# Fourier mixing and a hard-swish MLP on one core: batch 0's first two stages on the later batches' tables

## The chip, the cores and the metric

The kernel runs on one core of a Trainium2 chip. The core has five engines that run side by side and wait for one another by semaphores: TensorE (PE in the profile, with its weight loads listed as PEld), VectorE (DVE), ScalarE (ACT), GpSimd (POOL) and SyncE (SP). In this kernel SP only issues transfers (DMAs); ACT and POOL issue some too. The metric is the device time of one execution in microseconds. Three executions of the kernel before took 2608.43, 2608.70 and 2608.97 us; the median is 2608.7 us.

## The reference

```python
def _attn_ref(x, filt_r, filt_i):          # x: (8, 3008, 256), filters: (1505, 256)
    X = np.fft.rfft(x, axis=1)
    F = (filt_r + 1j * filt_i)[None, :, :]
    return np.fft.irfft(X * F, n=x.shape[1], axis=1).astype(np.float32)

def _moe_ref(x, w_in, w_out):              # x: (24064, 256), w_in: 256 x 2048, w_out: 2048 x 256
    h = x @ w_in
    g = h * np.clip(h + 3.0, 0.0, 6.0) / 6.0
    return (g @ w_out).astype(np.float32)
```

Each of the 8 batches is transformed along its 3008 rows, multiplied by one complex filter per frequency and channel, and transformed back. The 24064 rows that result go through a two-layer MLP with a hard swish. All is float32.

## The kernel before

3008 is 47 x 64, so a row number is written n = 64a + c with a < 47 (`NA`) and c < 64 (`NC`), and c = 32h + j with h in {0, 1} and j < 32 (`HC`). The forward transform has two stages. Stage A sums over a and leaves 24 residues k of the frequency (`KH`), real and imaginary. Stage B sums over c and leaves, for each k, 64 frequencies q. Then come the product with the filter (`f_unit`, on VectorE), the inverse of stage B (`bi_unit` on TensorE, copied out by ScalarE and stored to a scratch array `g_tmp`), and the inverse of stage A (`n_first`, `n_five`, `n_unit`, which read `g_tmp` back into `t4`). Their result is the ring `xn`, from which the MLP takes blocks of 512 rows: `plain_up` and `plain_down` for block 0, a form with fewer products for the others. The MLP fills TensorE for nearly all the time; the transform of batch n + 1 is put between the MLP steps of batch n by a written plan. Batch 0 has nothing to hide behind: its whole forward transform runs ahead of the MLP, and it is this opening, the first 64 us, that the change is about.

The opening is written out in order (a manual schedule: every engine gets its instructions in the order of the program text). In the kernel before:

- `x0_load` (L405) loads batch 0 into the upper part of the weight array `w_all` (`x0_at`), as 96 partitions (2a + h, starting at partition 16) in six transfers on SP (L1031). `start_t`, `wi_t` and the memsets of the 16 partitions below come first (L985 to L1023). ACT issues `start_t` as its first instruction.
- `keep_warm` (L1026) runs two products on zeros.
- `a0_unit(j)` (L417), for four values of j at a time and for each half of the 256 channels, runs four 112 x 128 x 128 products. The data are the stationary operand and one small table (`start`) the moving one; the table keeps the two h apart and has no factor that depends on j. One copy per half, on ACT or DVE, writes the results to `zt`, that is `xn` and `xs`.
- `table_load` (L255) loads the filter rows for four residues k (a chunk `c`, six chunks), in pieces of 32 partitions, and the chunk's part of a table `wb`, a 128 x 128 matrix for each k, which holds what stage A left out. Chunks 0 and 1 go to the tiles `ft0`, `ft1` and to `wa`; chunks 2 to 5 over `x0`, when stage A is through with it.
- `turn(c)` (L426) transposes eight 128 x 128 blocks of `zt` on TensorE; two copies bring them to `t2`.
- `b_unit(0, i)` (L532, L549) multiplies two k by their own 128 x 128 table into one PSUM bank; `f_unit(0, i)` (L552, L561 to L563) makes three DVE products; `bi_unit` (L577, L584) makes the inverse products of the chunk before, `g_store` stores them from POOL.
- For the last chunk `y_unit` combines the products, `direct` (L732) takes them straight to the first rows, `g0_first` (L621) and `first_load` (L659) carry the rest through `g_tmp`, and `n_first` (L736) ends the opening.
- Later `wa` (stage A's table for the later batches) and `wf` (their stage B table) are loaded, L1072, L1073 and L1084.

The conversions of the MLP weights (`w_load` L317, `w_conv` L327) are spread over the opening: transfers of 0.5 MB on SP, eight DVE instructions each for the first.

The transfers that SP and ACT issue share eight semaphores in turn, so an issue also waits until the transfer eight places before it has landed; SP issues strictly in order.

The later batches do stage A otherwise (`a_unit`, `a6_unit`): h = 0 lies on partitions 0 to 46 and h = 1 on 64 to 110, `wa` has 48 columns for each j with the j-dependent factors in it, four products run in the four quarters of the array, and DVE makes the sum and the difference of the two h. Their stage B (L540) then needs one table `wf` for all k, in pieces of 64 x 32.

## Time and profile before

| | |
|---|---|
| median of three executions | 2608.7 us |
| span of the profiled execution (first to last instruction) | 2607.0 us |
| around the span, to the median | 1.7 us |
| PE busy | 2591.8 us, 99% of the span |
| DVE busy | 2053.9 us, 79% |
| ACT busy | 1295.6 us, 50% |
| POOL busy | 486.7 us, 19% |
| start of `n_first` on PE | 61.62 us |
| moved by DMA in the first 61.6 us | 240 GB/s on average |

Times below are microseconds from the start of the span. In the timeline a line is a run of like instructions on one engine: start, duration, engine, line, operation, what it writes from what, partitions x elements, the number of records, and in brackets the idle time before it with what ended it. A float32 product makes two records. Idle time of PE is what costs, as PE is busy for 99% of the span; what stands in the opening shifts all that follows.

### The profile page before, as it was taken

Reading aid. Unit: us, or ns where it says so; the run is one execution under the profiler, and the core shown is the slowest. Engines: PE = TensorE matmul, PEld = TensorE weight load, DVE = VectorE, ACT = ScalarE, POOL = GpSimd, SP = SyncE. Lnnn points to the kernel's source line nnn. Section 1 sums busy time; section 2 is a strip of 40 time slices with the busy share of each in tenths; the row PEclk is TensorE's granted clock in tenths of the full one; section 3 lists DMA queues with packets and bytes.
Section 4 is the critical chain, followed back from the end, with each engine's and each line's share of the span. In section 5 each row is a group of like instructions: output and inputs, shape, how many; then the busy total and the mean of one; then the engine's idle time right before and its main releaser. Section 6 shows DMA issues by size and latency. Waiting matters only on the chain.

```text
span 2607.0 us, 86613 instructions
## 1 busy us (share of the span) xinstructions
PE 2591.8 (99%) x37708; PEld 2051.0 (79%) x37708; DVE 2053.9 (79%) x3611; ACT 1295.6 (50%) x2677; POOL 486.7 (19%) x711
## 2 busy tenths in 40 slices
PE   8999999999999999999999999999999999999999
PEld 6487777878778787788877888777877778888887
DVE  7978868888788877888778887788877888766666
ACT  4554454545545455444554444545445454455554
POOL 2242021121211202111031210311113120111110
PEclk9999999999999999999999999999999999999999
DMA  8732234112241132411224112331123321110000
GB/s 247 224 92 81 59 101 119 54 33 87 74 123 54 33 87 78 119 54 37 83 83 114 54 38 82 89 108 54 54 66 91 106 57 49 50 44 24 20 22 26
DMA packets 130834, 200.32 MB, mean 77 GB/s; under 512 B 21602, under 2 KB 97472, under 8 KB 130262
## 3 DMA queue, kind: packets, MB, share of 16 engines
q1 hardware_dynamic: 115165, 150.12, 20.4%
q0 software_dynamic: 14720, 44.16, 6.1%
q8 instruction: 296, 4.85, 0.8%
q14 instruction: 84, 0.69, 0.1%
q10 hardware_dynamic: 569, 0.50, 0.1%
HBM read 122.43 MB, written 83.98 MB: 79 GB/s over the span
## 4 chain that ended last, share of the span: by engine, by line
PE 94%; DVE 3%; DMA 2%; POOL 1%; issue 0%; ACT 0%; SPq 0%; POOLq 0%; DVEq 0%; ACTq 0%
PE po L765 43%; PE al L765 24%; PE be L765 18%; PE psn L705 2%; PE psf L540 1%; PE psf L481 1%; PE psf L600 1%; PE be L600 1%; POOL w_all L369 1%; PE be L481 1%; DVE g L818 1%; DMA g_tmp<-t 1%; PE psf L765 0%; DMA ft<-in_filt_i_dram 0%; DVE y L335 0%
## 5 line engine op out<-in xcount | busy, mean ns | idle before, releaser
L765 PEld LDWEIGHTS po<-w_all,g 128*64 128x64 f32 x20808 | 1232.5, 137 | 247.0 <-issue 12.4
L765 PE MATMUL po<-w_all,g 128*64 128x128 f32 (+1 forms) x20808 | 1407.0, 274 | 1.4 <-DVE g L818 0.7
L813 ACT ACTIVATE r<-h,half_c 128x512 f32<-128x512 f32 x736 | 531.0, 722 | 346.7 <-DVE h L794 334.7
L765 PE MATMUL al<-xt,w_all 128*64 128x256 f32 x4416 | 664.0, 379 | 0.4 <-POOL w_all L369 0.3
L818 DVE SCALAR_TENSOR_TENSOR g<-r,h 128x512 f32<-128x512 f32 x736 | 536.2, 730 | 144.6 <-ACT r L813 129.2
L765 PE MATMUL be<-xt,w_all 128*64 128x256 f32 x2944 | 442.6, 379 | 0.0
L794 DVE TENSOR_TENSOR h<-be,s 128x512 f32<-128x512 f32 x368 | 253.8, 690 | 131.3 <-PE be L765 102.2
L760 POOL TENSOR_TENSOR xt<-xn 128x256 f32<-128x256 f32 x184 | 150.7, 838 | 890.3 <-ACT xn L687 890.3
L765 PEld LDWEIGHTS be<-xt,w_all 128*64 128x64 f32 x2944 | 211.3, 137 | 106.5
L765 PEld LDWEIGHTS al<-xt,w_all 128*64 128x64 f32 x4416 | 278.9, 137 | 1.7 <-POOL w_all L369 1.4
L808 ACT ACTIVATE h<-al 128x256 f32<-128x256 f32 x368 | 141.4, 384 | 273.2 <-PE al L765 272.4
L826 DVE TENSOR_TENSOR g<-g 128x512 f32<-128x512 f32 x367 | 261.4, 712 | 12.6
L799 DVE TENSOR_TENSOR h<-al,s 128x256 f32<-128x256 f32 x368 | 156.0, 424 | 135.6 <-PE al L765 130.5
L789 ACT ACTIVATE s<-al 128x256 f32<-128x256 f32 x368 | 141.6, 385 | 207.2 <-PE al L765 207.1
L765 PE MATMUL al<-xn,w_all 128*64 128x256 f32 (+1 forms) x1536 | 240.1, 393 | 1.1 <-DVE g L818 0.7
L765 PE MATMUL be<-xn,w_all 128*64 128x256 f32 (+1 forms) x1536 | 236.4, 388 | 0.0
L780 ACT ACTIVATE s<-be 128x256 f32<-128x256 f32 x368 | 141.4, 384 | 170.1 <-PE be L765 170.1
L825 DVE TENSOR_TENSOR g<-g 128x256 f32<-128x256 f32 x367 | 165.5, 451 | 12.6
L779 ACT ACTIVATE s<-al 128x256 f32<-128x256 f32 x368 | 141.5, 384 | 59.1 <-PE al L765 59.1
L831 DVE TENSOR_TENSOR g<-g 128x256 f32<-128x256 f32 x367 | 161.7, 441 | 2.4
L765 PEld LDWEIGHTS be<-xn,w_all 128*64 128x64 f32 x1536 | 110.3, 137 | 62.3 <-issue 7.4
L506 POOL DMA_DIRECT2D z_tmp<-t x144 | 72.0, 508 | 321.4 <-ACT s L780 296.0
(162 smaller groups left out, 1766.6 us busy)
## 6 DMA issues: line engine op xcount, KB each, us to landing
t<-g_tmp SPq DMA_DIRECT2D x184, 120.0 KB
t<-z_tmp SPq DMA_DIRECT2D x42, 512.0 KB
g_tmp<-t POOLq DMA_DIRECT2D x68, 256.0 KB, 4.3
z_tmp<-t POOLq DMA_DIRECT2D x120, 144.0 KB, 3.7
o_tmp<-o SPq DMA_DIRECT2D x46, 256.0 KB
xs<-in_x_dram SPq DMA_DIRECT2D x60, 192.0 KB
ft<-in_filt_r_dram SPq DMA_DIRECT2D x168, 64.0 KB
ft<-in_filt_i_dram SPq DMA_DIRECT2D x168, 64.0 KB
```

The source lines that it names most:

```text
L760: nc.gpsimd.tensor_tensor(out=o, in0=x0, in1=x1, op=op_)
L765: nc.tensor.matmul(ps[ds(o, STRIP)], w[:, ds(o, STRIP)], x, skip_group_check=True, **kw)
L779: nc.scalar.activation(out=s[:, 0, :], in_=al, func=AXT.Copy)
L780: nc.scalar.activation(out=s5, in_=be[:, 1, :], func=AXT.Copy)
L789: nc.scalar.activation(out=s[:, 1, :], in_=al, func=AXT.Copy)
L794: nc.vector.tensor_tensor(out=st["h"][0].rearrange("p (a n) -> p a n", a=2), in0=be, in1=s, op=ALU.add)
L799: nc.vector.tensor_tensor(out=st["h"][1][:, 256:512], in0=al, in1=s5, op=ALU.add)
L813: nc.scalar.activation(out=r, in_=st["h"][i], func=AXT.Relu, bias=half_c, scale=1.0 / 6.0)
L818: nc.vector.scalar_tensor_tensor(out=st["g", k, p][:, o:o + 2, :].rearrange("p a n -> p (a n)"), in0=st["r", i], scalar=1.0, in1=st["h"][i ...
L825: v.tensor_tensor(out=g[:, G1, :], in0=g[:, G3, :], in1=g[:, G22, :], op=ALU.add)
L826: v.tensor_tensor(out=g[:, G3:G2 + 1:2, :], in0=g[:, G3:G1 + 1, :], in1=g[:, G11:G11 + 1, :].broadcast_to([P, 2, 256]), op=ALU.subtract)
L831: nc.vector.tensor_tensor(out=g[:, G4, :], in0=g[:, G12, :], in1=g[:, G2, :], op=ALU.subtract)
```

## The change

Batch 0's stage A uses `wa` and the four quarters of the array, as the later batches do; ScalarE copies the h = 0 sums to SBUF, and DVE makes even (add) and odd (subtract) sums. Stage B uses `wf`; `wb`, the second half of `start` and the fourth part of `wi` are gone. `x0` lies on partitions 0 to 46 and 64 to 110 and comes in four pieces a group, five groups, each with its columns of `wa`, which now are loaded here and not later. Filter rows come for two chunks at a time, in eight pieces of 16 partitions.

```diff
     def table_load(b, c):
-        if b == 0 and c >= FB:
-            at = x0_at(1536 * (c - FB), 1536)
-            t, wb = at[:, 0:1024].rearrange("p (k d) -> p k d", k=TC), at[:, 1024:].rearrange("p (k m) -> p k m", k=TC)
+        n = TC if b else 2 * TC
+        if b:
+            t = ft[(b * NT + c) % FB]
+            st["ft", b, c] = t
         else:
-            t, wb = ft[(b * NT + c) % FB], wa[:, ds(c % FB * TC * P, TC * P)].rearrange("p (k m) -> p k m", k=TC)
-        st["ft", b, c] = t
...
+            t = x0_at(2 * TC * D * (c // 2 - 1), 2 * TC * D).rearrange("p (k d) -> p k d", k=n) if c else ft_all
+            for i in range(2):
+                st["ft", b, c + i] = t[:, ts(i, TC), :]
         for src, p0 in ((filt_r, 0), (filt_i, HALF)):
-            nc.sync.dma_start(t[p0:p0 + 32, :, :].rearrange("p k d -> p (k d)"),
-                              raw(src, c * TC, [[NA * D, 32], [1, TC * D]]))
-            nc.sync.dma_start(t[p0 + 32:p0 + 64, :, :], raw(src, NA - c * TC, [[NA * D, 32], [-D, TC], [1, D]]))
-        nc.sync.dma_start(wb, wb_d[:, ts(c, TC), :])
-        st["wb", b, c] = wb
+            for r in range(2):
+                o = p0 + 32 * r
+                nc.sync.dma_start(t[o:o + 16, :, :].rearrange("p k d -> p (k d)"),
+                                  raw(src, c * TC + NA * r, [[2 * NA * D, 16], [1, n * D]]))
+                nc.sync.dma_start(t[o + 16:o + 32, :, :],
+                                  raw(src, NA * (2 - r) - c * TC, [[2 * NA * D, 16], [-D, n], [1, D]]))
...
-    def x0_load(j, n):
-        nc.sync.dma_start(x0[X0:XR, j:j + n, :].rearrange("p j d -> p (j d)"), raw(x[0], j, [[HC * D, XR - X0], [1, n * D]]))
+    def x0_load(j, n, q):
+        q.dma_start(wa[:, j * ATOM:(j + n) * ATOM + 16], wa_d[:, j * ATOM:(j + n) * ATOM + 16])
+        for h in range(2):
+            for r, m in ((0, 32), (32, NA - 32)):
+                nc.sync.dma_start(x0[h * 64 + r:h * 64 + r + m, j:j + n, :].rearrange("p j d -> p (j d)"),
+                                  raw(x[0], r * NC + h * HC + j, [[NC * D, m], [1, n * D]]))
...
-    def a0_unit(j):
+    def a0_unit(j, n):
         for dh in range(2):
-            ps = bank(0)
-            for u in range(4):
-                nc.tensor.matmul(ps[:, ts(u, P)], x0[0:XR, j + u, ts(dh, P)], st["start"][0:XR, ts(1, P)],
-                                 start=True, stop=True)
-            copy(dh and j not in (8, 12), zt(dh).rearrange("p (n j) -> p j n", j=HC)[:, j:j + 4, :],
-                 ps.rearrange("p (j n) -> p j n", j=4)[:, :, 0:4 * KH])
+            ps = [bank(0) for h in range(2)]
+            for u in range(n):
+                for g in range(2):
+                    for h in range(2):
+                        nc.tensor.matmul(ps[h][ts(g, HALF), ts(u, ATOM)], x0[ds(h * 64, NA), j + u, ds(dh * P + g * HALF, HALF)],
+                                         wa[ds(h * 64, NA), ts(j + u, ATOM)].rearrange("p (r x k) -> p k r x", r=2, k=2),
+                                         start=True, stop=True)
+            first = sp.tile([P, 512], FP32, name="s1")[:, 0:n * ATOM]
+            nc.scalar.activation(out=first, in_=ps[0][:, 0:n * ATOM], func=AXT.Copy)
+            for s_, op_ in ((0, ALU.add), (1, ALU.subtract)):
+                by_j = lambda t: t.rearrange("p (j q x) -> p j q x", j=n, x=NU)
+                nc.vector.tensor_tensor(out=zt(dh).rearrange("p (s q j x) -> p s j q x", s=2, j=HC, x=NU)[:, s_, j:j + n],
+                                        in0=by_j(first), in1=by_j(ps[1][:, 0:n * ATOM]), op=op_)
 
     def turn(c):
...
-                    k = c * TC + 2 * v + u
-                    nc.tensor.transpose(ps[:, ds(u * D + dh * P, P)], zt(dh)[:, ts(k, P)], st["start"][:, 0:P])
+                    z = zt(dh).rearrange("p (s r x) -> p s x r", s=2, x=NU)[:, s_, 2 * c + v, :]
+                    nc.tensor.transpose(ps[:, ds(s_ * D + dh * P, P)], z, st["start"][:, 0:P])
...
     def b_unit(b, i):
         c, r = divmod(2 * i, TC)
-        if b > 1:
+        if b != 1:
             t = st.pop(("t2", b, c))
             ps = [bank(b) for k in range(2)]
...
-        nc.scalar.dma_start(st["start"][:, 0:2 * P], start_d)
         zero = rp.tile([P, 512], FP32, name="r", tag="r")
-        nc.vector.memset(x0[0:X0, 0:4, :], 0.0)
-        nc.gpsimd.memset(x0[0:X0, 4:8, :], 0.0)
...
-        nc.scalar.dma_start(wi, wi_d)
...
-        for j, n, bits in (0, 4, 0), (4, 4, 0), (8, 8, 1), (16, 8, 1), (24, 4, 1), (28, 4, 1):
-            x0_load(j, n)
-            load_bits(bits)
+        groups_0 = (0, 4), (4, 4), (8, 8), (16, 8), (24, 8)
+        for j, n in groups_0:
+            x0_load(j, n, nc.sync if j else nc.scalar)
+            load_bits(j >= 8)
+            if j == 4:
+                nc.scalar.dma_start(st["start"][:, 0:P], start_d)
+        nc.sync.dma_start(wf, wf_d)
         table_load(0, 0)
+        nc.sync.dma_start(wi, wi_d)
         load_bits(2)
-        table_load(0, 1)
-        for j in range(0, HC, 4):
-            a0_unit(j)
-            convert(j == 4)
+        for j, n in groups_0:
+            a0_unit(j, n)
+            convert(j == 8)
         nc.gpsimd.memset(t4, 0.0)
-        for c in range(FB, NT):
+        for c in range(FB, NT, 2):
             table_load(0, c)
...
             for i in (2 * c, 2 * c + 1):
-                b_unit(0, i)
+                if i % 2 == 0:
+                    b_unit(0, i)
                 f_unit(0, i)
...
-        nc.sync.dma_start(wa[:, 0:528], wa_d[:, 0:528])
-        nc.sync.dma_start(wf, wf_d)
...
-            nc.sync.dma_start(wa[:, 528:], wa_d[:, 528:])
```

The code that makes the tables changes with it (the frequencies of a chunk stand in the order that `wf` gives). Stages of the later batches issue the same instructions as before.

## The prediction

> **What bounds the kernel now.** I read the page first, then the opening engine by engine in the timeline, then the chain that ended last within it. The page's slices: PE is full in all but the first.
>
> ```profile
> PE   8999999999999999999999999999999999999999
> DMA  8732234112241132411224112331123321110000
> ```
>
> PE works for 2591.8 of 2607.0 us, so about 15 us are to be had in all; most of them lie in the first 64. Only there can the change act, and what it shifts there shifts everything behind. The timeline of PE and DVE, opening:
>
> ```profile
> 3.02 3.78 PE L1028 MATMUL al<-r 128*128 128x512 f32 x4 [3.02 <-ACT r L1022]
> 6.59 15.48 PE L421 MATMUL po<-p,w_all 112*128 112x128 f32 x128
> 22.96 0.33 PE L433 MATMUL al<-p,xs 128*128 128x128 f32 x1 [0.53 <-DVE xs L413]
> 24.20 1.99 PE L549 MATMUL po<-t,wa 128*128 128x256 f32 x8 [0.25 <-ACT t L415]
> 51.16 1.81 PE L732 MATMUL psn<-w_all,t 128*128 128x470 f32 x4 [1.02 <-ACT t L587]
> 61.62 1.85 PE L765 MATMUL psn<-wai,t 128*64 128x94 f32 x40 [0.80 <-DMA t<-g_tmp]
> ```
> ```profile
> 25.36 0.69 DVE L561 TENSOR_TENSOR s<-po,ft 128x512 f32<-128x512 f32 x1 [0.69 <-PE po L549]
> 42.78 0.69 DVE L561 TENSOR_TENSOR s<-po,w_all 128x512 f32<-128x512 f32 x1 [0.29 <-PE po L549]
> 47.51 0.69 DVE L561 TENSOR_TENSOR h<-po,w_all 128x512 f32<-128x512 f32 x1 [0.46 <-issue]
> ```
>
> Stage A keeps PE without a gap from 6.59 to 22.07: the loads run ahead of it. From 25.36 DVE makes filter products (4.29 us a chunk) with only the two gaps shown, so PE's 4.66 us a chunk hardly counts: DVE already sets this stretch. The end of the opening, 61.62, waited 0.80 for `g_tmp` to come back. What feeds it, on SP and ACT, and the shape of the chain:
>
> ```profile
> 0.75 1.34 SPq L406 DMA_DIRECT2D w_all<-in_x_dram  x3
> 17.38 0.33 SPq L277 DMA_DIRECT2D ft<-in_filt_r_dram  x1
> 1.17 1.28 ACT L991 ACT_TABLE_LOAD   x1 [1.17 <-PEq L1274]
> 2.77 0.33 ACTq L1023 DMA_DIRECT2D wi<-wi_t  x1
> ```
> ```profile
> 49.87 0.37 ACT t L587
> 50.98 4.56 DMA g_tmp<-t
> 58.19 3.34 DMA t<-g_tmp
> ```
>
> L277 at 17.38 is the issue that waited for the last piece of x0 (eight places before it), so x0 was in at about 17.4. In the stretches table (last columns: granted clock, DMA share, GB/s) DMA is full from 18 to 46:
>
> ```profile
> 18.00:28.00 10.00, 8.60 (x63) 7.49 (x62) 5.71 (x8) 3.84 (x6) 0.00 (x0) 1.00 0.95 248
> 28.00:46.00 18.00, 18.00 (x96) 11.09 (x94) 17.10 (x26) 7.93 (x14) 3.56 (x6) 1.00 0.98 296
> 90.00:97.00 7.00, 6.53 (x114) 3.30 (x110) 6.62 (x12) 3.54 (x6) 0.00 (x0) 1.00 0.73 222
> ```
>
> **The change, part by part.** The same forms run later in the trace, so their prices can be read:
>
> ```profile
> 95.15 1.38 PE L705 MATMUL psn<-wai,t 48*64 48x47 f32 x80
> 426.65 1.09 PE L540 MATMUL psf<-t,wf 64*32 64x512 f32 x16
> ```
>
> 1. Stage A on PE. L705 is the same shape as the new products: 40 quarter products in 1.31 us to the next start, 0.131 us per four. The change has 256, 64 fours: 8.4 us instead of 15.5. But it gains only where PE was the bound, and after the change loading is.
>
> 2. Loading x0. Before x0's last piece there stood 3.15 MB of x0, 0.52 of weights, 0.13 of `start` and 0.13 of `wi`: 3.93 MB from about 1.9 to 17.4, 0.254 MB/us. Now it is 3.08 of x0, 0.81 of `wa`, 0.52 and 0.07: 4.49 MB, 17.7 us at that rate, so 19.6 if the queue never empties. It does, I think. Group j of `wa` takes columns 48j to 48(j + n) + 16, so each load overlaps the one before by 16 columns, and each must wait for it to land. `wa`'s first group is no longer ACT's first act: it stands behind the 1.28 us table load and two activations, at about 2.4. Its landing: `start`, issued at 0.75, let PE's weight load start at 5.74; `wi`, issued at 2.77, was in by 6.67; the `g_tmp` piece took 3.3 us. With 3.0 us it is in at 5.4; only then can SP issue `wa`'s second group and x0's. The third waits again, another 3.0: 8.4. So the first group (0.49 MB) moves until about 4, the second from 6.7 to 8.6, and the third's bytes start near 9.7 (0.4 an issue, and 1.2 to the first bytes, as x0's start at 0.75 with bytes from 1.9 shows): some 4 us of the queue stand empty. The remaining 3.4 MB take 12.1 to 13.4 us (0.28 to 0.254), and x0 is in at 22 to 23; I take 23 because there are more pieces, 0.42 us of SP each. The pieces of 32 and 15 partitions ran at 222 GB/s with DMA only 0.73 busy at 90 to 97, where SP issued each 0.42 us; that would make it 25 as the upper end. Lower end: 19.6, no idling. The fourth and fifth waits lie behind 1.3 MB of queued loads and cost little.
>
> 3. Stage A's end. Last group: 16 fours, 2.1 us; ACT's copy of 384 elements about 0.5 (0.38 for 256, 0.60 for 512); two DVE sums of 384 at 0.56 (0.42 for 256, L799; 0.69 for 512). 23 + 2.1 + 0.5 + 1.1 = 26.7, against first full transposes at 22.96. Sums for the earlier groups and the one conversion (4.4 us) lie in the gaps of loading; DVE's whole work here is 14.0 us (8 x 0.36 + 12 x 0.56 + 4.4) in the 20 from the first group's landing, so it is not the bound. `st["start"]` and the memsets go, at no gain: other engines waited for neither but PE's start at 5.74.
>
> 4. To the first filter product. Before: 2.40 us from 22.96 to 25.36. Now one call makes both banks of the chunk and needs both halves of `t2`, the second being DVE's copy: + 0.5. First product: 26.8 + 2.9 = 29.7, + 4.3. The filter rows for it, 1.05 MB in 16-partition pieces behind x0 and `wf`, need 5.7 us at the 0.21 MB/us that 17.4 to 27.5 had: 28.7, just hidden; late by a microsecond per 0.2 MB if the loads slip further. Chunk 2's rows have 8.6 us more.
>
> 5. Chunks. PE now needs 0.87 (transposes) + 1.03 (L540) + 1.87 (inverse) = 3.8 per chunk, under DVE's 4.29. The gaps of 0.29 and 0.46 close: - 0.7. The last chunk starts at 51.1 instead of 47.51, + 3.6. That is all stage B can give: VectorE's work in it is the same.
>
> 6. Tail. `direct` and the last inverse on PE follow + 3.6; they would have let `n_first` start at 60.82 but for the `g_tmp` wait, so 64.4. By the store: ACT's copies of chunk 4 were held to 49.87 by an earlier store, not by DVE, which had its products at 47.04; now they come about 3 later, and 11.7 us on (49.87 to 61.53) it is 64.5. So + 2.8.
>
> 7. Behind it. `wa` (0.79 MB) and `wf` leave SP's queue at 59.5 to 73; no PE gap there hangs on them alone (the wait at 97.20 is 0.67 for `xs`, behind conversions). 0, at best - 0.7. The rest is the same code.
>
> Sum: + 2.8 on the span of 2607.0, 2609.8. The profiled span stands 1.7 under the median 2608.7; with the same around it, 2611.5.
>
> **Where a rule of the skill speaks.** Trace first: `keep_warm`'s four 512-column passes take 3.78 us, two such passes, side by side, later 0.47 (L584); stage A's first four products took 1.95 us (ACT's first copy 8.54), later ones 0.89, while the granted clock reads 1.00. So PE starts at half speed until about 9. The Trainium skill, "TensorE: Matmul & The Clock Gate", Part 1, says PE falls back to half after some 3.4 us without work. By that rule gaps of 3 to 4 us between x0's groups would leave stage A's end cold; no stretch of this trace has such a gap. By the rule the sum is rival C's, without it A's. My sum goes by full speed, as every row behind 9 us shows it.
>
> **Rivals.**
> - A, as summed: 2611.5, own range 2609.5 to 2613.5. For it: the overlap of `wa`'s columns is in the text. 0.45.
> - B, the loads never idle (the other side): the waits land in 2 us each and the queue stays full. x0 in at 17.7 to 19.6. Break-even is x0 in at 20.2: then the first product comes at 26.9, + 1.5, less 0.7 and the 0.8 of slack. At 18.5 the end is 1.2 to 1.7 earlier: about 2607.5. For it: SP had 2.9 MB out by 5.6; against it: the order of SP's queue. 0.20.
> - C, PE is at half speed again at the end of stage A: last group + 2.1, transposes + 0.9, first stage B + 1.0 on top of A: 2615.5; if the last two groups back to back warm it, 2613. For it: the half-speed start; against it: groups follow each other every 3 to 4 us. 0.20.
> - D, strided reads cost: the transposes now read every twelfth element, the new products every second of `wa`. No PE row has this; the nearest are copies with 128-byte steps (384 elements 0.83 on DVE against 512 plain in 0.69: 1.6 times an element) as the upper end, 1.0 as the lower. I take 1.0 in A; with 1.6 the chunk on PE is 4.3, level with DVE, and stage A's end and first transposes gain 1.6: 2613. 0.15.
>
> **Numbers.** A change under 0.2% (5.2 us) is about what a measurement here cannot tell from none. Faster than 2603.5 needs more than B's best: 0.02. Slower than 2613.9: most of C, a third of D, A's edge: 0.22. The rest 0.76. The range, 2607 to 2616, holds B's middle and C.
>
> **What the profile after would show.** A: SP's second `wa` issue near 5, its third near 8; stage A on PE in five bursts with gaps of 2 to 4 us; first filter product at 29 to 30; chunks 4.3 apart; `n_first` near 64.4. B: first product before 27. C: the last burst of stage A (16 fours, 128 records) lasting 4 us, not 2. D: transposes over 1.2 us a chunk. Wrong would also be a wait behind 64 us that is not there before, or filter rows that land after 30.

## The result, and the profile after

The changed kernel takes 2621.26 us (median of 4 runs, 2620.14 to 2622.10) against 2608.56 for the kernel before in the same comparison: a ratio of 1.0050, 95% interval 1.0035 to 1.0064. It is 12.7 us slower. The prediction was 2611.5 with a range that ended at 2616.

The profiled execution after took 2622.1 us with a span of 2620.3. Its page has the same PE share as before, 99%. In PE's row only the first slice differs; the DMA digits differ by one here and there, along the whole run:

```profile
PE   7999999999999999999999999999999999999999
DMA  8742244212342123421224212241133421110000
```

The first of PE's 40 slices fell from 8 to 7; that is 65 us in which PE worked less. All of the loss lies there. A landmark behind it, the start of each of the 368 operations on DVE that make `h` from `be` and `s` in the MLP steps, comes 13.3 us later than before at the first one (129.98 us before) and 12.4 to 13.2 later at all others; the span ends 13.4 later. So what happened is over by 75 us, and the rest of the run only carries it along.

The opening on PE, from the timeline of the kernel after (start, busy us, line, what, count, and in brackets the idle time before and what ended it):

```profile
6.24 1.53 PE L394 MATMUL po<-wa,w_all 47*64 47x48 f32 x64
9.37 1.14 PE L394 MATMUL po<-wa,w_all 47*64 47x48 f32 x62 [0.68 <-DMA w_all<-in_x_dram]
14.99 3.66 PE L394 MATMUL po<-wa,w_all 47*64 47x48 f32 x126 [1.67 <-DMA w_all<-in_x_dram]
22.01 4.11 PE L394 MATMUL po<-wa,w_all 47*64 47x48 f32 x128 [0.59 <-DMA w_all<-in_x_dram]
27.90 4.00 PE L394 MATMUL po<-wa,w_all 47*64 47x48 f32 x126 [1.79 <-DMA w_all<-in_x_dram]
33.13 0.49 PE L411 MATMUL al<-p,xs 128*128 128x128 f32 x1 [0.81 <-DVE xs L401]
35.78 1.96 PE L518 MATMUL po<-t,wf 64*32 64x512 f32 x16 [0.83 <-issue]
46.26 1.09 PE L518 MATMUL po<-t,wf 64*32 64x512 f32 x16
63.96 2.30 PE L709 MATMUL psn<-w_all,t 128*128 128x470 f32 x4 [2.45 <-issue]
```

Stage A's five groups are to be seen (32 fp32 products of the program are 64 records, a group of eight `j` is 128). Each group waited for its rows, and the last one for rows that came at 27.9. The bursts of 126 and 128 records take 3.7 to 4.1 us, 29 to 32 ns a record, where the first ones took 18 to 24. One form in two places tells why: stage B's 16 records of L518 take 1.96 us at 35.78 and 1.09 at 46.26. PE runs at half its speed: the clock records of the trace have it fall at 10.54 us, behind gaps of no more than 0.68 us, and come back at 44.68. The windows, with the granted clock (the share of TensorE's full clock), the DMA share and GB/s at their end, say the same and show what the loads did:

```profile
12.00:24.00 12.00, 6.49 (x206) 6.12 (x208) 5.63 (x12) 0.98 (x2) 0.00 (x0) 0.50 0.88 198
24.00:36.00 12.00, 8.46 (x206) 7.14 (x209) 5.33 (x10) 2.56 (x5) 0.00 (x0) 0.50 1.05 187
36.00:44.00 8.00, 7.31 (x48) 3.41 (x33) 5.70 (x9) 1.78 (x3) 0.00 (x0) 0.50 0.96 165
```

In the same three stretches the kernel before had a clock of 1.00 throughout and moved 266, 229 and 327 GB/s. After, the DMA engines are about as full, at 165 to 198 GB/s; only from 18 to 22 us, while SP was held, they were 0.66 and 0.50 busy. On SP's queue the fifth `wa` load, which shares 16 columns with the fourth, was held from 13.30 to 19.85, and x0's last pieces went out behind it:

```profile
11.12 0.35 SPq L373 DMA_DIRECT2D wa<-wa_t  x1
19.85 0.34 SPq L373 DMA_DIRECT2D wa<-wa_t  x1
20.24 2.26 SPq L376 DMA_DIRECT2D w_all<-in_x_dram  x4
```

What follows on DVE is the old pace with a later start; the last sums of stage A, the first filter product and the last chunk's:

```profile
32.52 1.02 DVE L401 TENSOR_TENSOR xs<-s,po 128x384 f32<-128x384 f32 x2 [1.05 <-ACT s L398]
37.81 0.69 DVE L538 TENSOR_TENSOR s<-po,ft 128x512 f32<-128x512 f32 x1 [2.14 <-PE po L518]
42.39 0.69 DVE L538 TENSOR_TENSOR h<-po,ft 128x512 f32<-128x512 f32 x1 [0.32 <-PE po L518]
60.30 0.69 DVE L538 TENSOR_TENSOR h<-po,w_all 128x512 f32<-128x512 f32 x1
```

The first product is 12.45 us later than the 25.36 of before, the last chunk 12.79, `n_first` (at 74.89) 13.27. So nearly all of the loss is there by the first filter product: 9.83 us of it is the end of stage A on PE (31.90 against 22.07), 2.62 the way from there to the product.

### The profile page after: what moved, and what is told of

Its sections match the earlier page's. It is cut to its first block, busy times and chain, and to the rows that moved or that the text cites. A ratio compares the mean times of both kernels' runs of the same rounds, so it can differ in the third digit from the quotient of the medians.

```text
span 2620.3 us, 87529 instructions
## 1 busy us (share of the span) xinstructions
PE 2593.8 (99%) x38140; PEld 2047.6 (78%) x38140; DVE 2055.2 (78%) x3624; ACT 1290.3 (49%) x2677; POOL 480.9 (18%) x707
## 4 chain that ended last, share of the span: by engine, by line
PE 96%; DMA 2%; DVE 1%; issue 0%; SPq 0%; ACT 0%; POOL 0%; POOLq 0%; DVEq 0%; ACTq 0%
PE po L742 44%; PE al L742 25%; PE be L742 18%; PE psn L682 2%; PE psf L518 1%; PE psf L459 1%; PE psf L577 1%; PE be L577 1%; PE be L459 1%; DMA wa<-wa_t 1%; PE psf L742 0%; DMA g_tmp<-t 0%; PE psf L432 0%; DVE g L795 0%; PE psn L742 0%
## 5 line engine op out<-in xcount | busy, mean ns | idle before, releaser
L742 PEld LDWEIGHTS po<-w_all,g 128*64 128x64 f32 x20808 | 1233.6, 137 | 245.5 <-issue 12.4
```

Source lines behind the costliest of these rows:

```text
L742: nc.tensor.matmul(ps[ds(o, STRIP)], w[:, ds(o, STRIP)], x, skip_group_check=True, **kw)
```

## The experiments

In the tables "stage A ends" is the end of its last product on PE, "first product" the start of DVE's first filter product, both in the profiled execution; executions of one kernel lie up to 3 us and more apart, so medians a microsecond apart are not told apart.

### One suspect at a time: the overlap, PE's speed, narrow pieces

The first four asked which of the prediction's doubts had come true: the overlap of `wa`'s loads (e1), PE at half speed (e2: four dummy products of 512 columns behind groups 2, 3 and 4 and one behind group 5), both (e3); and, from the other side, what narrow pieces alone do to the kernel before (e4: each x0 transfer of before cut in three of 32 partitions).

```diff
 e1, e3
-        q.dma_start(wa[:, j * ATOM:(j + n) * ATOM + 16], wa_d[:, j * ATOM:(j + n) * ATOM + 16])
+        end = (j + n) * ATOM + (16 if j + n == HC else 0)
+        q.dma_start(wa[:, j * ATOM:end], wa_d[:, j * ATOM:end])
 e2, e3
             a0_unit(j, n)
+            keep_warm({0: 0, 4: 4, 8: 4, 16: 4, 24: 1}[j])
 e4, in the kernel before
-        nc.sync.dma_start(x0[X0:XR, j:j + n, :].rearrange("p j d -> p (j d)"), raw(x[0], j, [[HC * D, XR - X0], [1, n * D]]))
+        for r in range(0, XR - X0, 32):
+            nc.sync.dma_start(x0[X0 + r:X0 + r + 32, j:j + n, :].rearrange("p j d -> p (j d)"),
+                              raw(x[0], r * HC + j, [[HC * D, 32], [1, n * D]]))
```

> The changed kernel, with each group's load of wa cut to its own 48n columns (the 16 extra columns go with the last group alone), so that no load of wa waits for the one before. Waits (the queue stands empty while SP waits 9.1 us for wa): SP's last x0 issue comes at about 14 instead of 22.5. If the waits were all that is wrong with loading, x0 is in at 19.6 to 20.5 instead of 27.8 and the opening ends 7 to 8 us earlier, time about 2613.5. Narrow pieces (x0's pieces of 32 and 15 partitions and the filter rows' of 16 move at 0.15 to 0.18 MB/us with DMA fully busy, waits or not): 3.08 MB at 0.17 and 1.4 MB of wide loads at 0.35 give x0 in at about 24, 4 us earlier, time about 2617. Clock (PE at half speed from 11 to 45 is what costs): no more than 1 us earlier, 2620 to 2621.

> The changed kernel with four of keep_warm's products on zeros after the second, third and fourth group of stage A on PE and one after the fifth; loads as they were. Clock: PE stays at full speed, the granted clock reads 1.00 after 12; the last burst takes 2.1 us instead of 4.0, the way from first transposes to the first filter product 2.9 instead of 4.7, the gaps of 0.32 and 0.79 on DVE close: opening 4 to 5 us shorter, time about 2617. Waits or narrow pieces alone: x0 still in at 27.8, no change, 2620 to 2622. If the slow PE is due to the strided reads of the new products and transposes and not to the clock: bursts still 4 us, no change.

> Both of these together. Waits and clock as the whole cause: x0 in at 20, first filter product near 27, opening 12 us shorter, time 2609 to 2610, level with before. With narrow pieces as a third cause: x0 in at 24, first product near 30, time 2612 to 2614. If the two overlap (earlier data keep PE warm by themselves): as the run without overlap, within 1 us.

> The kernel before, with each of its six x0 transfers of 96 partitions cut into three of 32 partitions; same bytes, same places, nothing else. Narrow pieces: 3.15 MB at 0.175 and 0.8 MB of wide loads at 0.35 put x0 in at about 22 instead of 17.4; stage A then waits for loads and ends 3 to 4 us later; time 2611.5 to 2613. Waits alone: no loss, 2608 to 2609, as the 18 issues of 0.35 to 0.42 us take no longer than the bytes.

| kernel | time, us (range) | ratio to before, 95% | stage A ends | first product | n_first |
|---|---|---|---|---|---|
| before | 2608.81 (2607.38 to 2610.73) | | 22.07 | 25.36 | 61.62 |
| after | 2621.26 | 1.0050 (1.0035 to 1.0064) | 31.90 | 37.81 | 74.89 |
| e1, no overlap | 2623.20 (2622.66 to 2624.25) | 1.0057 (1.0042 to 1.0072) | 34.11 | 40.02 | 76.90 |
| e2, dummies | 2619.73 (2618.17 to 2620.71) | 1.0043 (1.0028 to 1.0058) | 31.03 | 35.61 | 72.98 |
| e3, both | 2620.31 (2619.21 to 2622.47) | 1.0046 (1.0031 to 1.0061) | 30.37 | 34.94 | 70.94 |
| e4, before with narrow x0 | 2612.47 (2610.87 to 2613.74) | 1.0013 (1.0003 to 1.0023) | 24.68 | 27.98 | 64.97 |

The overlap is not it: without it SP has x0 out by 20.1 instead of 22.5, yet the last group waited for its rows until 28.61, and stage A ends later. Of e1's end, 0.76 and 1.59 us are stops in the middle of groups, for which the profile names no releaser; what they are comes out below:

```profile
28.61 2.38 PE L395 MATMUL po<-wa,w_all 47*64 47x48 f32 x78 [1.21 <-DMA w_all<-in_x_dram]
32.58 1.53 PE L395 MATMUL po<-wa,w_all 47*64 47x48 f32 x48 [1.59 <-issue]
```

The dummies did bring PE back to full speed (timeline of e2, two of the bursts that had taken 4.1):

```profile
17.19 2.08 PE L394 MATMUL po<-wa,w_all 47*64 47x48 f32 x128
22.83 2.13 PE L394 MATMUL po<-wa,w_all 47*64 47x48 f32 x128
```

and still stage A ended at 31.0. Its rows were as late as without the dummies (the issue of SP that waits for the last piece of x0 stands at 28.03, at 27.78 in the kernel after), and the dummies ahead of the last group ran until it started, at 28.52. e4 has the narrow pieces alone: they cost the kernel before 2.6 us at the first filter product and 3.7 on the median, with the DMA share at 1.00 to 1.03 and 229 to 234 GB/s from 4 to 20 us, where before it had 266 to 292 behind 8 us. Not all of that is rows: behind e4's one gap in stage A PE ran at half speed from 12.71 to 16.12, which is 1.7 of the 2.6.

```profile
12.05 12.63 PE L423 MATMUL po<-p,w_all 112*128 112x128 f32 x96 [2.04 <-DMA w_all<-in_x_dram]
```

Nine more are to be explained.

### Rows by whole transfers, two queues

If late rows were the loss, rows that come in wide transfers must take it away. e5 loads 96 partitions in one transfer a group (the last 32 are zeroed), e6 does the same for the filter pairs (128 partitions), e7 is e6 without overlap and with the dummies. Other data reach the products; sizes, forms and order stay. e8 keeps the data and has GpSimd issue half of x0's pieces.

```diff
 e5, e6, e7
-        for h in range(2):
-            for r, m in ((0, 32), (32, NA - 32)):
-                nc.sync.dma_start(x0[h * 64 + r:h * 64 + r + m, j:j + n, :].rearrange("p j d -> p (j d)"),
-                                  raw(x[0], r * NC + h * HC + j, [[NC * D, m], [1, n * D]]))
+        nc.gpsimd.memset(x0[96:P, j:j + n, :], 0.0)
+        nc.sync.dma_start(x0[0:96, j:j + n, :].rearrange("p j d -> p (j d)"), raw(x[0], j, [[HC * D, 96], [1, n * D]]))
 e6, e7
+        if not b:
+            nc.sync.dma_start(t.rearrange("p k d -> p (k d)"), raw(filt_r, 0, [[n * D, P], [1, n * D]]))
+            return
 e8
-                nc.sync.dma_start(x0[h * 64 + r:h * 64 + r + m, j:j + n, :].rearrange("p j d -> p (j d)"),
+                (nc.sync, nc.gpsimd)[h].dma_start(x0[h * 64 + r:h * 64 + r + m, j:j + n, :].rearrange("p j d -> p (j d)"),
```

> The changed kernel, but each group of x0 comes in one transfer of 96 partitions (0 to 95, rows of the kernel before, partitions 96 to 127 set to zero by GpSimd) in place of four narrow ones; the transform of batch 0 is therefore of other data, with the same work. wa keeps its overlap. Narrow pieces: x0 moves at 0.27 to 0.29 MB/us; with the waits of SP for wa about 5 us remain, x0 in at 20 to 22 instead of 27.8; filter rows in 16-partition pieces still move at 0.16, so they are in at 28 to 29 and the first filter product comes near 29.5 to 30; time 2612 to 2614. If the number of pieces, and not their width, made the rate, the same. If the waits for wa were the cause after all: x0 in at 26 or later, time 2619 to 2621.

> As the run before it, and each pair of filter chunks comes in one transfer of 128 partitions (other rows, the same bytes) in place of eight of 16. Narrow pieces: the filter rows are in 4 us after x0 and are no longer what the first product waits for; it comes when stage A and the transposes are through, 27 to 29 with PE at half speed; 0 to 1.5 us less than the run before, time 2611 to 2613. Filter pieces harmless: the same as the run before.

> Wide transfers for x0 and filters, no overlap in wa, and keep_warm's products between the groups: all three suspected costs gone. If they are all there is, x0 is in at 18 to 19, the first filter product comes at 24.5 to 26 and the opening is at least as short as before: time 2606.5 to 2609. If something else of the change costs (the strided reads, the split sums on DVE), 2611 or more.

> The changed computation whole, no overlap in wa, keep_warm's products between the groups, and x0's pieces of h = 1 (partitions 64 to 110) issued by GpSimd instead of SP, so that pieces for both halves of the partitions are under way together. If narrow pieces are slow one by one but two halves can move at once: x0 in at 19 to 21 instead of 27.8, time 2611 to 2614. If the 16 DMA engines are held by a narrow piece whichever queue it comes from: DMA still 0.16 to 0.18 MB/us, time 2619 to 2621 as with one queue.

| kernel | time, us | ratio to before, 95% | stage A ends | first product | n_first |
|---|---|---|---|---|---|
| e5, wide x0 | 2621.69 (2619.80 to 2622.37) | 1.0050 (1.0035 to 1.0065) | 30.83 | 36.63 | 72.66 |
| e6, and wide filter rows | 2619.94 (2619.13 to 2621.28) | 1.0045 (1.0030 to 1.0060) | 31.64 | 37.43 | 74.62 |
| e7, and no overlap, dummies | 2621.39 (2619.75 to 2622.50) | 1.0050 (1.0035 to 1.0065) | 34.12 | 38.71 | 74.73 |
| e8, two queues, no overlap, dummies | 2621.79 (2620.10 to 2622.19) | 1.0050 (1.0033 to 1.0067) | 35.76 | 40.35 | 75.04 |

Wide rows did come earlier: e5's last group started at 24.86, 3.0 us before that of the kernel after. But a stop in the middle of it took more than half of that back:

```profile
24.86 2.71 PE L392 MATMUL po<-wa,w_all 47*64 47x48 f32 x84 [1.08 <-DMA w_all<-in_x_dram]
29.32 1.52 PE L392 MATMUL po<-wa,w_all 47*64 47x48 f32 x44 [1.75 <-issue]
```

None of the four helps in time, and that was the turn of the study: with wide, unheld loads and PE at full speed from the third group on, e7's stage A ended at 34.1. In e7 PE had no gap from 10.7 to 35.2 but one of 0.72, and 13 dummies filled what the rows had left free. So the dummies were in the way now, and the next run took them out.

### The wide kernel without dummies: a third limit

f1 is e7 without dummies; f3 adds four dummies ahead of stage A, where PE has nothing to do (6.3 to 10.7). f2 and f4 are the same pair with the real rows: x0 in two transfers of 64 partitions a group, 17 of each unused.

```diff
 f2, f4
-            for r, m in ((0, 32), (32, NA - 32)):
-                nc.sync.dma_start(x0[h * 64 + r:h * 64 + r + m, j:j + n, :].rearrange("p j d -> p (j d)"),
-                                  raw(x[0], r * NC + h * HC + j, [[NC * D, m], [1, n * D]]))
+            nc.sync.dma_start(x0[ts(h, 64), j:j + n, :].rearrange("p j d -> p (j d)"),
+                              raw(x[0], h * HC + j, [[NC * D, 64], [1, n * D]]))
 f3, f4
-        keep_warm(2)
+        keep_warm(6)
```

> The kernel after with the table's loads cut apart, batch 0's rows in transfers of 96 partitions (the last 32 zeroed) and its filter pairs in one transfer of 128 partitions: other rows reach the products, so the output is another one; no dummy products between the groups of stage A, which the wide kernel with dummies had on its path (four of them took 4.7 us from 14.9, and stage A then ran without a gap from 10.7 to 35.2). Theory 1 (late, narrow transfers and a PE at half speed make up the loss): the first group starts near 10.7 and takes 4.2, the others 2 to 3 each behind one another; stage A ends at 21 to 24, the first filter product comes at 25 to 28 and n_first at 61 to 65, the time is 2608 to 2612. Theory 2 (stage A with its four bursts, copies and sums cannot end before about 30 however its data come): n_first stays at 72 or later, the time at 2617 or more.

> The kernel after with the table's loads cut apart and each half of batch 0's rows in one transfer of 64 partitions instead of one of 32 and one of 15; the 17 rows more that each brings are not used, and the computation is whole. It moves 4.2 MB for x0 instead of 3.1. If the number of partitions sets the rate (theory 1, between the 180 GB/s of the pieces and the 290 of the wide transfers), the last rows are in at 20 to 24, stage A ends at 25 to 28, n_first is at 65 to 69 and the time 2611 to 2616. If bytes alone count (the rate stays at 180), x0 is later than in the kernel with the loads cut apart, and the time 2622 or more.

> The wide kernel without overlap, and four more dummy products ahead of stage A's first group, in the gap from 6.3 to 10.7, where nothing waits for PE. If the granted speed of PE in stage A is a part of the loss, the first group takes 2.1 instead of 4.2 and the time is 1.5 to 3 below the same kernel without the four; if stage A follows its data, it is the same within 0.7.

> The kernel with x0 by 64 partitions and the same four dummy products ahead of the first group. The first rows come at about 6.5 there, so that the four, 3.4 to 5 us, may lie on the path of the first group; the later groups wait for their data. Expected between 1 below and 1 above the same kernel without them if the data set the pace, 2 or more below it if the speed of PE does.

| kernel | time, us | ratio to before, 95% | stage A on PE | first product |
|---|---|---|---|---|
| f1, wide, no overlap | 2622.45 (2621.55 to 2623.83) | 1.0055 (1.0040 to 1.0070) | 11.07 to 34.17 | 40.02 |
| f2, real rows by 64 | 2624.92 (2623.43 to 2625.74) | 1.0065 (1.0049 to 1.0082) | 7.20 to 34.66 | 40.45 |
| f3, f1 and early dummies | 2623.50 (2622.34 to 2624.50) | 1.0059 (1.0044 to 1.0074) | 11.18 to 33.91 | 39.80 |
| f4, f2 and early dummies | 2626.60 (2624.90 to 2627.78) | 1.0070 (1.0055 to 1.0085) | 10.62 to 39.06 | 44.85 |

The theory of rows and clock was wrong by 8 us and more on f1 and f2, and the early dummies did not help: f3 is level with f1, f4 is 1.7 us slower than f2. In f3 PE was at full speed from 6.26 us, but only to 13.09. The timeline of f1 shows what the theory lacked:

```profile
11.07 4.28 PE L396 MATMUL po<-wa,w_all 47*64 47x48 f32 x130 [4.75 <-DMA wa<-wa_t]
15.65 2.59 PE L396 MATMUL po<-wa,w_all 47*64 47x48 f32 x85 [0.30 <-DVE xn L403]
22.12 4.00 PE L396 MATMUL po<-wa,w_all 47*64 47x48 f32 x127 [3.88 <-issue]
28.84 5.33 PE L396 MATMUL po<-wa,w_all 47*64 47x48 f32 x170 [2.73 <-issue]
```

Two things. PE is busy from 11.07 to 18.24 with one rest of 0.30 us and stays at 30 to 33 ns a record: its own stage A does not bring it to full speed. And it then stands still for 3.88 and 2.73 us with "issue" as the cause: for no semaphore, in the middle of a group. Counted from the start, weight loads and products together, the two gaps stand before PE's 449th and 705th record, 256 apart. In the trace's DMA records a packet of 16384 bytes on the queue of kind "instruction" precedes each; some of these stops, and two packets without one:

```
kernel  gap before record  packet of 16384 B     PE goes on  after the packet
f1      449                19.34 to 20.61        22.12       1.51
f1      705                26.32 to 27.39        28.84       1.45
f3      449                18.91 to 20.17        21.69       1.52
f3      705                25.60 to 26.68        28.18       1.50
f4      705                27.96 to 29.47        30.99       1.52
e8      449                18.80 to 19.93        21.76       1.83
e7      705                24.87 to 25.89        27.34       1.45
e1      961                29.49 to 31.11        32.57       1.46
e5      961                26.03 to 27.63        29.32       1.69
after   961 (no gap)       27.31 to 28.72        30.37       1.65
before  449 (no gap)       20.02 to 21.11        39.11       18.0
```

16384 bytes for 256 instructions are 64 bytes each. The new stage A has 256 products, each two weight loads and two products in the trace: 1024 instructions, four such blocks, where the old one's 64 products had 256. At full speed a block is used up in 2.1 us, at half in 4.2; from PE's 449th record to the packet for the block behind it (22.12 to 26.32 in f1) went 4.2 us while the DMA engines were full, 1.1 the packet, 1.5 until PE went on. The Trainium skill, "Runtime: NRT & Kernel Launch", Instruction fetch mechanics, has the same blocks of 16 KiB or 256 instructions, and says that crossing a block's border is mostly hidden; the kernel before agrees (its block was there 18 us early), f1 with 3.88 and 2.73 us of standstill does not.

The kernel after has no such gap, but by little: its 961st record ran 1.65 us behind its packet, no later than the stopped ones did. Rows and instructions were late together there.

### Half of the products

If instructions are the limit, half as many must free stage A. g1 joins each two products of 64 columns to one of 128, in f1; g3 does it in e1; g2 adds four dummies to g1. g4 asks the kernel before whether its own products cost by the columns that move: 96 instead of 128. (The expectation for g3 says that e1 had no wait at a multiple of 256. It had two, 0.76 us before the 705th record and 1.59 before the 961st.)

```diff
 g1, g2, g3
-                for g in range(2):
-                    for h in range(2):
-                        nc.tensor.matmul(ps[h][ts(g, HALF), ts(u, ATOM)], x0[ds(h * 64, NA), j + u, ds(dh * P + g * HALF, HALF)],
+                for h in range(2):
+                    nc.tensor.matmul(ps[h][:, ts(u, ATOM)], x0[ds(h * 64, NA), j + u, ts(dh, P)],
 g2
+            keep_warm({0: 0, 4: 2, 8: 1, 16: 1, 24: 0}[j])
 g4, in the kernel before
-                nc.tensor.matmul(ps[:, ts(u, P)], x0[0:XR, j + u, ts(dh, P)], st["start"][0:XR, ts(1, P)],
+                nc.tensor.matmul(ps[:, ds(u * P, 4 * KH)], x0[0:XR, j + u, ts(dh, P)], st["start"][0:XR, ds(P, 4 * KH)],
```

> The wide kernel without overlap (other rows, output another one), with each pair of 64-column products of stage A joined into one of 128 columns: 128 products instead of 256, and with two weight loads and two products each 512 PE instructions instead of 1024. In the kernel that it is made from, PE stood still for 3.88 us before its 449th and for 2.72 us before its 705th instruction, 256 apart, each time 1.5 us after a 16 KB packet of the instruction queue had landed. Theory 3 (PE waits for its instructions, which come in blocks of 256 behind the data): these two gaps go, stage A ends at 26 to 30 instead of 34.2 and the time is 2613 to 2619, 4 to 8 below the same kernel with 256 products; PE's work is the same if a product of 128 columns takes twice one of 64, and less if it does not. Theory 1 (clock and data alone): the end of stage A stays within 1.5 of 34 and the time at 2621 to 2624.

> The same kernel with half the products, and dummy products that keep PE at full speed: two behind the second group, one behind the third and one behind the fourth (0.85 us each at full speed, 1.9 at half, 16 instructions in all). If the granted speed of PE is what is left of the loss, stage A ends 3 to 5 earlier than without the dummies, transposes and stage B's first products take half their time, and the time is 2610 to 2614. If the data come too late for that, it is within 1 of the kernel without them.

> The kernel after with the table's loads cut apart and stage A in 128 products of 128 columns; the computation is whole, x0 comes in its narrow pieces. With the loads cut apart alone the time was 2623.2 and stage A ended at 34.1. There no wait at a multiple of 256 instructions was seen, and each group waited for its rows. If the late rows set the pace, stage A's end moves by less than 2 and the time stays at 2621 to 2624; if the number of instructions does, it falls to 2615 to 2619.

> The kernel before with stage A's products over the 96 columns that are used, not over 128. Its stage A ran without a gap from 6.6 to 22.1, 0.111 us for each record. If the columns set that time, a record takes 0.083 and stage A ends at 18.5 to 19.5 (x0 is in at 17.4); the time falls by 2 to 3, to 2606. If the weight loads of 128 columns set it, nothing changes.

| kernel | time, us | ratio to before, 95% | stage A on PE |
|---|---|---|---|
| g1 | 2628.42 (2627.52 to 2628.67) | 1.0078 (1.0063 to 1.0093) | 11.17 to 39.06 |
| g2 | 2635.15 (2634.99 to 2635.52) | 1.0105 (1.0088 to 1.0122) | 10.58 to 46.35 |
| g3 | 2623.77 (2623.36 to 2624.81) | 1.0062 (1.0047 to 1.0077) | 6.24 to 34.59 |
| g4 | 2608.12 (2607.25 to 2621.16; before 2607.85) | 1.0010 (0.9999 to 1.0020) | 6.60 to 22.28 |

The times missed, but every "issue" gap in stage A is gone with the instructions, in g1, g2 and g3. What took its place is PE itself. The whole of g1's stage A is one burst of 27.90 us (the window of the line ends at 36), and g2's is cut only by its dummies (timelines of g1, then g2):

```profile
11.17 25.16 PE L395 MATMUL po<-wa,w_all 47*128 47x48 f32 x232 [4.85 <-DMA wa<-wa_t]
```
```profile
10.58 7.07 PE L395 MATMUL po<-wa,w_all 47*128 47x48 f32 x64 [4.26 <-DMA wa<-wa_t]
17.58 3.78 PE L999 MATMUL al<-r 128*128 128x512 f32 x4
21.29 7.07 PE L395 MATMUL po<-wa,w_all 47*128 47x48 f32 x64
```

107 ns a record on average, for 28 us on end. g3's first 32 records took 56 to 58 each, before its PE fell to half speed, so 107 is half speed; g2's two dummies together did not end it (3.78 us for four passes is half speed too), and its four dummies, 7.9 us, cover the 6.7 that it lost on g1. And a record of 128 columns takes 107 ns where two of 64 took 66 in f1, so joining them costs PE 10 us at half speed instead of nothing. g4 did nothing: a record of 96 columns took the 0.111 of 128, so it is not the moving columns that set the old stage A's time.

### Full speed in the wide kernel, bought with more or fewer dummies

The last two ask the question that was left: does full speed help once the rows are early? Both are f3 with dummies between the groups, h1 seven and h2 three.

```diff
 h1
+            keep_warm({0: 1, 4: 1, 8: 2, 16: 2, 24: 1}[j])
 h2
+            keep_warm({0: 0, 4: 1, 8: 1, 16: 1, 24: 0}[j])
```

> The wide kernel without overlap and with the four early dummy products (other rows, output another one), and between stage A's groups 1, 1, 2, 2 and 1 dummy products of 0.93 us at full speed. Before this, a group's 128 recorded products took 2.1 at full speed (16 ns between two) and 4.2 at half (33). Theory 4 (stage A of this form runs at half speed unless other products keep PE fast, and that half, with the late rows and the waits for instructions, is the loss): all groups take 2.1, together 8.4; with 6.5 of dummies behind the start at 11 and up to 5 of waits for instructions stage A ends at 26 to 31, n_first comes at 67 to 71 and the time is 2613 to 2619. Against it: the groups at full speed and the time still at 2621 or more.

> The same kernel with fewer dummy products: none, 1, 1, 1 and none. If one of 0.93 us between groups is enough to keep PE fast, stage A ends 2 to 4 before that of the kernel with seven, at 23 to 28, and the time is 2610 to 2616; if it is not, the groups fall back to 33 ns between two products, stage A ends at 31 to 34 and the time is 2619 to 2623.

h1 took 2620.26 us (2619.15 to 2620.97), 1.0045 (1.0030 to 1.0060); h2 2624.31 (2622.27 to 2625.63), 1.0063 (1.0046 to 1.0080). Stage A ended at 33.64 and 33.52, f1's at 34.17 and f3's at 33.91. The dummies bought full speed in part: 18 to 25 ns a record in the first and last groups, 29 to 34 from 14.4 to 23.4 in h1 and from 21.8 to 27.6 in h2. So the expectation that all groups take 2.1 missed; but where PE was fast, it did not end sooner. From the timeline of h2, the third group's start and the runs of records behind the stops in its third, fourth and fifth group:

```profile
16.33 1.64 PE L396 MATMUL po<-wa,w_all 47*64 47x48 f32 x77
21.82 1.73 PE L396 MATMUL po<-wa,w_all 47*64 47x48 f32 x51 [3.85 <-issue]
28.08 1.02 PE L396 MATMUL po<-wa,w_all 47*64 47x48 f32 x54 [0.47 <-issue]
32.45 1.07 PE L396 MATMUL po<-wa,w_all 47*64 47x48 f32 x58 [0.80 <-issue]
```

And of h1, with more dummies, behind the first two of these stops:

```profile
21.69 1.74 PE L396 MATMUL po<-wa,w_all 47*64 47x48 f32 x53 [1.01 <-issue]
28.40 1.13 PE L396 MATMUL po<-wa,w_all 47*64 47x48 f32 x58 [0.53 <-issue]
```

Four dummies fewer, 3.6 us more of standstill (5.1 against 1.5), the same end. The packets came at 19.1, 25.9, 29.5 and 34.2 in h1, at 19.1, 25.6, 30.0 and 33.5 in h2, at 19.3, 26.3, 30.3 and 33.8 in f1: the blocks of instructions keep nearly the same time, whether PE is slow (f1), in part fast or busy with something else, and PE waits for them. e7, at full speed from 19.4 on, had them at 18.3, 24.9, 28.7 and 33.9, with its 13 dummies in place of the waits. In the wide kernels that is the bound; and it is why faster rows gave nothing.

No version came out ahead of the kernel before; g4, the only one level with it, is the kernel before in all that counts. That stage A can be freed of all three limits at once was not shown: fewer instructions were had only with products that keep PE slow.

## Why the prediction was wrong

Its steps against the two profiles (us; "end of the sums" is DVE's last addition or subtraction of stage A):

| step | before | predicted | after |
|---|---|---|---|
| 2, x0's last rows let PE start | 17.4 | 23 | 27.90 |
| 1, the last group on PE | | 2.1 long | 4.00 long |
| 3, end of the sums | | 26.7 | 33.54 |
| 4, first filter product | 25.36 | 29.7 | 37.81 |
| 5, last chunk's first product | 47.51 | 51.1 | 60.30 |
| 6, n_first | 61.62 | 64.4 | 74.89 |

- **Step 2, loading x0, is the term that was sized wrong most: 4.9 us.** It blamed the overlap of `wa`'s columns for the idle queue and said that the fourth and fifth waits "cost little". The fifth was the longest (6.5 us of SP), but without any overlap (e1) the rows were no earlier. What it did not price was the pieces: it moved the last 3.4 MB at 0.254 to 0.28 MB/us, rates of 96-partition transfers; they took from 9.7 to 27.9, 0.19 MB/us, with the DMA engines full but for 18 to 22 us. Its upper end, 25 at the 222 GB/s of pieces of 32 and 15 partitions, came from a stretch in which DMA was 0.73 busy and stores to `z_tmp` moved too. e4 confirms the direction (+ 2.6 us at the first filter product for pieces of 32 alone, 1.7 of them by PE's speed behind the gap), and wide rows in e5 let the last group start at 24.86. Whether it is the width of the pieces or their number that costs, no run separates.
- **Step 1 held only at full speed.** 16 ns a record, the 8.4 us of the prediction for the whole, was measured in e2 and e3, with dummies. Alone, stage A fell to 29 to 33 ns. It cost 1.9 us in the last group.
- **Step 3's copies and sums were right:** 1.64 us from PE's end to DVE's, predicted 1.6. **Step 4** was 1.3 short, 4.27 against 3.0, for transposes (0.22 a record instead of 0.11) and stage B at half speed. The three misses, 4.9, 1.9 and 1.3, make the 8.1 between 29.7 and 37.81.
- **Steps 5 and 6** gave 1.1 and 1.3 more. DVE's gaps did not close, they became 0.32 and 0.79, since PE's first chunks at half speed were 4.6 us apart; in the rest of the stretch DVE had no gap, and stage B's form gained nothing. `direct`'s first passes, behind 2.45 us of rest, took 2.30 and 2.63 instead of 1.81 and 1.77. Together 10.5 of n_first; the medians differ by 9.8 from the prediction. **Step 7** was right: nothing is gained or lost behind 75 us.
- **Rival C had the mechanism,** PE at half speed at the end of stage A, and its mark, a last burst of 4 us. Its price, 4.0 on top of A, was about right for what it covers (1.9, 1.3 and some of the 2.4 behind); it lacked the late rows. The reason against it, that groups follow each other every 3 to 4 us, was no reason: PE fell to half speed with no gap above 0.68 us in the 3.4 us before, stayed there with gaps of at most 2.4 in stage A, and in g1 with none. **Rival B** fell: the queue did idle, but full it was no faster. **Rival D** is small: at full speed (e2) transposes of every twelfth element come 0.128 apart instead of 0.109, 1.0 a chunk, hidden by DVE.
- What neither the sum nor a rival had: the number of PE instructions. In the kernel after it costs nothing that can be seen, but it stands level with the rows (1.65 us from packet to use), and where the rows came earlier it took back what they gave (1.75 us of standstill in e5, 6.6 in f1). No run brought stage A's end below 30.37 (e3).

The Trainium skill, "TensorE: Matmul & The Clock Gate", Part 1, was cited in the prediction for a fall to half speed after some 3.4 us without work, and it says that some 3.4 us of sustained work bring full speed. Here the fall came sooner: in the kernel after at 10.54 us, with gaps of 0.63 and 0.68 us in the 3.4 before. And in f1 7.2 us of records with one rest of 0.30, in g1 28 us without any, did not bring full speed. So by these runs it is not enough that PE has a record running; products of 47 rows and 48 columns do not count as the 112-row, 128-column ones of before do, which were at full speed from 8.7 us on. What it is in them that counts is not shown.

## What to carry to other kernels

Price a stage that is cut into more and smaller products by its instructions too: a block of 256 that PE uses up faster than the next one is brought (6.7 us from one stop to the next in f1, with the DMA queues full) will be waited for, and the profile calls that wait "issue". When an ablation of one limit gives nothing, look at what PE waits for in the ablated kernel and not at the time alone; three limits (rows, speed, instructions) hid one another here, and only the runs without the first showed the third. And take a transfer rate from a stretch with full DMA engines and pieces of the same number and width.

## What the runs showed of the hardware

- PE at half speed without a gap: 107 ns a record instead of 56 for 28 us (g1), 33 instead of 16 for 7 us (f1). Four dummies of 512 columns behind a group brought full speed and kept it (e2, e3, e7; in e8 it was lost again for 3.4 us behind a stop of 2.71); one or two did so in part (h1, h2), and two behind a slow group of 128-column products not at all (g2).
- The granted clock of a window that lies ahead of the trace's first clock record reads 1.00 whatever PE does. g1's windows show 1.00 from 12 to 36 us, g2's 0.50, with the same 107 to 110 ns a record; but g1's first clock record stands at 51.81 (f1's at 41.92, that of before at 8.72), and there its speed changes: stage B's 16 records take 1.96 us at 47.11 and 1.09 at 53.21. Behind the first record the two agree (g2: 1.00 from 6.24 to 9.65, then 0.50).
- A block of 256 PE instructions comes as one packet of 16384 bytes, which took 0.9 to 1.7 us; PE goes on 1.3 to 1.8 us after it. Behind full DMA queues the packet comes 3.2 to 5.4 us after the request that PE's progress suggests (the kernel after, f1), with quieter ones (f1 behind 28.84, 0.50 busy) 1.4. The request itself is not in the trace, so this part is inferred.
- Stretches of x0's pieces of 32 and 15 partitions and the filter rows' of 16 moved 165 to 198 GB/s at a DMA share of 0.88 to 1.05; the same stretches of the kernel before, with transfers of 32 to 128 partitions, 229 to 327. Pieces of 64 (f2) left the last group's start at 29.6, no earlier than the narrow ones with 27.9 for three quarters of the bytes. What a second issuing engine gives is not shown: e8's half of the rows that GpSimd issued had landed by 19.6 us, but its dummies and a stop of 2.71 us stood in the way.
